# Linear attention and a routed two-layer network on one core: the first layer put ahead of the last routing step, subtractions moved to GpSimd, row loads and one output tile placed earlier

## The chip, the cores and the metric

The kernel runs on one core of a Trainium2 chip. A core has five engines that run side by side and meet through semaphores: TensorE (PE in the rows; its weight loads are PEld), VectorE (DVE), ScalarE (ACT), GpSimd (POOL) and SyncE (SP), which here only asks for transfers. The metric is the device time of one execution in microseconds.

## The reference

Attention with a feature map, then a mixture of eight experts with one expert for each token. Cut to what is computed:

```python
def phi(x):                                   # x: 4 x 8 x 576 x 64
    proj = einsum('bhsd,df->bhsf', x, w_phi)  # 128 features
    proj = proj - max(abs(proj), axis=-1)
    return concatenate([exp(proj), exp(-proj)], axis=-1)
kv, z = einsum('bhsf,bhsd->bhfd', phi(k), v), sum(phi(k), axis=2)
x = einsum('bhsf,bhfd->bhsd', phi(q), kv) / (einsum('bhsf,bhf->bhs', phi(q), z) + 1e-6)
# tokens: x as 2304 rows of 512
logits = x @ w_gate; e = argmax(logits); gate = softmax(logits)[e]
pos = how many earlier tokens chose e         # kept while pos < 576
h = maximum(rows_of_e @ w1[e], 0)             # 512 -> 1024
out = gate * (h @ w2[e])                      # 1024 -> 512
```

With this input the experts get 73, 516, 236, 236, 170, 250, 418 and 405 tokens.

## The kernel before

**Attention** goes through 72 items (`items`), 36 for each half of the tokens: a K item or a Q item is 128 tokens times four heads. `attention()` is a software pipeline written out by hand: in its step `t` every item that is in flight gets one stage. TensorE projects (L243, L244), VectorE takes the largest absolute value (L249) and subtracts it (L253, `center`), TensorE transposes a Q item (L329), ScalarE takes both exponentials (L331, L332), TensorE sums (L315 for K, L344 for Q), and `rows_out` divides by the sum. Nothing reorders this: each engine runs its instructions in the order in which the program emits them. Beside it, in later steps, ScalarE rounds the first expert's first-layer weights (`w_split`, L110, tile `h`), and VectorE or GpSimd takes the rest (L111, tile `l`): a product of two such pairs needs three matmuls. `x_split` does the same for the Q and K inputs (L179 on GpSimd).

**Routing** is done for groups of 9, 4, 3 and 2 blocks of 128 tokens (`route`). Its some twenty small steps lie in the queue `pending`, and `tick()` emits one or two of them between the large VectorE operations. After the first group thirteen more steps (`swaps`, L449 to L461) find the expert that leads so far and put it first. `positions` (L422) counts on TensorE. When a group is through, each block's rows are scattered to their expert's place in `xs` in DRAM (L426, an indirect transfer by GpSimd).

**Experts.** `prep` transposes a tile of 128 rows (L673, tile `pt`), ScalarE rounds it (L674), VectorE takes the rest (L675). `ffn1(f)` is the first layer for 128 of the 1024 hidden columns (L740, L741, L743), `relu` its result (L754, L757), `ffn2` the second layer for one tile of rows (L771, L773, L774; `py_t`, in the rows `pt` or `sm`), `put` scales it and scatters it to the output (L786, L153). `opening` begins with the leading expert, whose first 256 rows are surely there; `totals` (L907 to L913) writes the counts `cnt`, `count(e)` loads a count into a register of every engine, and branches choose the path: over 256 rows, over 128 (`to_two`), or fewer (`to_one`, which computes 128 rows with `thin1`). The second expert here has 73 rows and goes `to_one`, the four after it `to_two`. The first output tile of an expert (`first`) is computed behind the branch of the next one. `told` is a hint on where a branch will go. `loads` asks for the next expert's weights (L106, tile `raw`) and rows (L663, tiles `xi` and `xr`) from SyncE's queue, in which a request that waits holds up those behind it. `paced` ties a request to the latest VectorE operation.

Of the kernel before, what the change touches and what calls it, by code (L numbers as in the profile page):

```python
# [8 lines left out]
F32 = mybir.dt.float32  # L9
# [28 lines left out]
def tile_kernel(ctx: ExitStack, tc: tile.TileContext, qT, kT, vT, vv, w_phi, w_g, w1, w2, out, cap):  # L38
# [23 lines left out]
                   allow_small_or_imprecise_dtypes=True)  # L62
    tokid = cpool.tile([P, NT // P], I32, tag="tokid", name="tokid")
# [44 lines left out]
    def w_split(c, part, low=None):  # L108
        a, hi, lo = (t[:, :, part * P:(part + 1) * P] if c < 2 else t[:, part] for t in (raw_t[c], *w_t[c]))
        nc.scalar.activation(hi, a, AF.Copy)  # L110
        (low or nc.vector).tensor_tensor(lo, a, hi.bitcast(F32), ALU.subtract)  # L111
# [273 lines left out]
    def route(blk, n, xr, lg):  # L385
# [59 lines left out]
        def swaps():  # L445
# [7 lines left out]
                lambda: v.tensor_scalar(lead, lead8, float(NE), None, ALU.add),  # L453
                lambda: v.tensor_scalar(perm["h"], iota8, lead8, None, ALU.is_equal),
                lambda: v.tensor_scalar(perm["b"], perm["h"], lead, None, ALU.mult),
                lambda: v.tensor_scalar(perm["c"], iota8, float(-NE), lead, ALU.is_equal, ALU.mult),
                lambda: v.tensor_tensor(perm["d"], perm["c"], perm["b"], ALU.subtract),
                lambda: v.scalar_tensor_tensor(perm["e"], perm["d"], float(NE), iota8, ALU.add, ALU.add),
                lambda: v.tensor_scalar(perm["s"], perm["e"], float(slots), None, ALU.mult),
                lambda: v.tensor_copy(perm_i, perm["e"]),  # L460
                lambda: v.tensor_copy(seen_i, seen),  # L461
# [93 lines left out]
    def attention():  # L555
# [46 lines left out]
        depth = 8  # L602
        for t in range(len(items) + depth):
# [57 lines left out]
    def load_x(e, t0, t1, after):  # L661
        for s0, m in tiles[t0:t1]:
            dma = nc.sync.dma_start(xi_t[e % 2, s0][0:m], xs[e * slots + s0:e * slots + s0 + m, :])  # L663
            for w in after:
# [125 lines left out]
    def first(e):  # L790
        ffn2(wide, *tiles[0], 0)
        put(e, *tiles[0], 0)

    def ready(e):
        for t in tiles[:2]:
            prep(e, *t)
# [213 lines left out]
```

## Time and profile before

| what | us |
|---|---|
| median of 3 runs | 471.55 |
| lowest and highest run | 470.67 and 472.55 |
| the profiled execution | 467.43 |
| its span, first to last instruction | 465.7 |
| TensorE busy in the span | 412.6 (89%) |
| VectorE, ScalarE, GpSimd busy | 274.3, 245.6, 165.3 |

The profiled execution is 4.1 us (0.9%) under the median, and 1.7 us of it lie outside its span. Attention fills the span up to some 177 us, the opening goes to 220 us, the experts to 458 us. In the rows below a time is counted from the start of the span; an entry in square brackets is how long the engine sat idle before the row, and what ended that wait.

### The profile page before, as it was taken

The numbers are of one execution on the slowest core, as the hardware profiler recorded it, in microseconds if no ns is written. First come the engines' busy times: TensorE is split into PE (matmuls) and PEld (weight loads), VectorE is DVE, ScalarE is ACT, GpSimd is POOL, SyncE is SP. The second block draws the span as 40 slices with busy tenths as digits, with TensorE's granted clock in tenths as the row PEclk, the third lists the DMA queues.
The fourth block names the chain that finished last, engine by engine and source line by source line (L and its number), as shares of the span: only waits on it lengthen the run. The fifth ranks groups of instructions, "written<-read, shape, count | busy, mean of one in ns | idle before, by whom it ended". The sixth has DMA issues, their size and how long they took to land.

```text
span 465.7 us, 12137 instructions
## 1 busy us (share of the span) xinstructions
PE 412.6 (89%) x4777; PEld 362.9 (78%) x4777; DVE 274.3 (59%) x606; ACT 245.6 (53%) x453; POOL 165.3 (35%) x194
## 2 busy tenths in 40 slices
PE   6989999959998775846999599998989999999992
PEld 4778888848887664835988579896979899889872
DVE  5768887898976885521205857575656565165410
ACT  3879687667955663501215755554655554164310
POOL 1667486144677546000004510414123140042011
PEclk9999999998999997977999979999999999999997
DMA  7961698568056423195000769585775829310010
GB/s 266 383 258 45 209 368 288 198 212 292 10 168 199 161 112 152 56 333 164 24 24 27 249 241 309 193 307 201 259 240 208 304 73 326 115 34 24 0 48 27
DMA packets 42717, 82.80 MB, mean 178 GB/s; under 512 B 4351, under 2 KB 9343, under 8 KB 42624
## 3 DMA queue, kind: packets, MB, share of 16 engines
q1 hardware_dynamic: 38080, 72.13, 45.0%
q0 software_dynamic: 4544, 9.47, 5.8%
q8 instruction: 54, 0.88, 0.8%
q14 instruction: 39, 0.32, 0.2%
HBM read 62.65 MB, written 24.30 MB: 187 GB/s over the span
## 4 chain that ended last, share of the span: by engine, by line
PE 49%; DMA 4%; ACT 1%; issue 1%; POOLq 0%; SPq 0%; DVE 0%; POOL 0%; ACTq 0%
PE ph L741 7%; PE ph L743 7%; PE ph L740 7%; PE sm L771 5%; PE sm L773 4%; PE sm L774 4%; PE pt L771 3%; PE pt L773 3%; PE pt L774 3%; DMA xi<-xs 2%; PE pt L673 2%; DMA xr<-xs 2%; PE pt L769 1%; PE pt L767 1%; PE ph L718 1%
## 5 line engine op out<-in xcount | busy, mean ns | idle before, releaser
L179 POOL TENSOR_TENSOR stk<-px,stk 64x1024 f16<-64x1024 f32 (+1 forms) x30 | 70.8, 2361 | 58.7 <-ACT stk L178 58.1
L111 DVE TENSOR_TENSOR l<-raw,h 128x512 fp32r<-128x512 f32 x124 | 82.6, 701 | 8.4 <-ACT h L110 5.2
L153 POOL DMA_INDIRECT out<-y,it x22 | 21.6, 981 | 171.6 <-ACT y L786 95.5
L740 PE MATMUL ph<-xh,h 128*128 128x256 f32 (+3 forms) x272 | 76.5, 305 | 0.6 <-issue 0.6
L741 PE MATMUL ph<-xh,l 128*128 128x256 f32 (+3 forms) x272 | 76.2, 304 | 0.0
L110 ACT ACTIVATE h<-raw 128x512 fp32r<-128x512 f32 x128 | 74.6, 626 | 0.0
L757 DVE SCALAR_TENSOR_TENSOR h<-ph,h 128x256 fp32r<-128x256 f32 (+1 forms) x88 | 32.5, 392 | 54.8 <-ACT h L754 52.8
L754 ACT ACTIVATE h<-ph 128x256 fp32r<-128x256 f32 (+2 forms) x64 | 27.6, 431 | 60.5 <-PE ph L743 59.9
L249 DVE TENSOR_REDUCE m<-pr 128x4 f32<-128x512 f32 x72 | 49.2, 684 | 8.2 <-PE pr L244 4.7
L740 PEld LDWEIGHTS ph<-xh,h 128*128 128x128 f32 x272 | 52.8, 194 | 1.5 <-issue 0.6
L741 PEld LDWEIGHTS ph<-xh,l 128*128 128x128 f32 x272 | 52.9, 195 | 0.9
L253 DVE TENSOR_TENSOR d<-pr,m 128x512 f32<-128x512 f32 x72 | 49.8, 691 | 3.9
L743 PE MATMUL ph<-xh,h 128*128 128x256 f32 (+3 forms) x272 | 49.1, 303 | 0.0
L243 PE MATMUL pr<-whi,stk 128*128 128x128 f16 x260 | 37.0, 223 | 12.5 <-DVE d L253 11.6
L315 PE MATMUL acc<-v,kp 128*64 128x73 f32 (+1 forms) x1280 | 46.2, 234 | 0.4 <-issue 0.4
L315 PEld LDWEIGHTS acc<-v,kp 128*64 128x64 f32 (+1 forms) x1280 | 40.7, 140 | 5.0 <-issue 1.2
L344 PE MATMUL acc<-kv,qp 128*64 128x73 f32 x1152 | 44.5, 229 | 0.0
L344 PEld LDWEIGHTS acc<-kv,qp 128*64 128x64 f32 x1152 | 39.1, 136 | 6.0 <-issue 5.7
L743 PEld LDWEIGHTS ph<-xh,h 128*128 128x128 f32 x272 | 41.2, 195 | 0.7
L675 DVE TENSOR_TENSOR xh<-pt,xh 128x512 fp32r<-128x512 f32 (+1 forms) x23 | 14.9, 677 | 43.1 <-ACT xh L674 43.1
L771 PE MATMUL sm<-h,h 128*128 128x512 f32 x88 | 35.4, 403 | 3.2 <-ACT h L110 1.8
L244 PE MATMUL pr<-wlo,stk 128*128 128x128 f16 x260 | 36.5, 221 | 0.0
(143 smaller groups left out, 748.2 us busy)
## 6 DMA issues: line engine op xcount, KB each, us to landing
raw<-in_w SPq DMA_DIRECT2D x28, 1024.0 KB, 7.3
xs<-fill SPq DMA_DIRECT2D x18, 514.0 KB, 5.4
xr<-xs SPq DMA_DIRECT2D x24, 257.0 KB, 8.2
raw<-in_w SPq DMA_DIRECT2D x8, 512.0 KB, 4.3
vt<-in_vT SPq DMA_DIRECT2D x3, 1152.0 KB, 13.2
v<-in_vv SPq DMA_DIRECT2D x2, 1314.0 KB, 12.1
px<-in_kT SPq DMA_DIRECT2D x5, 512.0 KB, 9.5
px<-in_qT SPq DMA_DIRECT2D x4, 640.0 KB, 11.1
```

The costliest lines, as they stand in the source:

```text
L110: nc.scalar.activation(hi, a, AF.Copy)
L111: (low or nc.vector).tensor_tensor(lo, a, hi.bitcast(F32), ALU.subtract)
L179: return lambda: nc.gpsimd.tensor_tensor(t[other], x, t[own], ALU.subtract)
L243: nc.tensor.matmul(pr[:, j], lt, whi, start=True, stop=False)
L249: nc.vector.tensor_reduce(m.rearrange("p a b -> p (a b)"), pr, AX.X, ALU.max, apply_absolute_value=True)
L253: beat[0] = nc.vector.tensor_tensor(d, pr, m.to_broadcast([P, 4, NF]), ALU.subtract)
L315: nc.tensor.matmul(acc[f:f + D, a, j * GC:(j + 1) * GC], kp[lo:hi, j, a, f:f + D], vt[lo:hi, r, h * GC:(h + 1) * GC], start=first and j == ...
L344: nc.tensor.matmul(num[lo:hi, g, j * GC:(j + 1) * GC], qp[:, a, j, lo:hi], kv_t[b][:, a, 4 * g + j], start=(a == 0), stop=(a == 1))
L740: nc.tensor.matmul(acc, hi[:, k, fs], xh[:, k, o:o2], start=(k == 0), stop=False)
L741: nc.tensor.matmul(acc, lo[:, k, fs], xh[:, k, o:o2], start=False, stop=False)
L743: nc.tensor.matmul(acc, hi[:, k, fs], xl[:, k, o:o2], start=False, stop=(k == 3))
L771: nc.tensor.matmul(py[0:m], h_t[f][:, s0:s0 + m], hi, start=(f == 0), stop=False, skip_group_check=True)
```

## The change

Six things are moved. (1) Nine of the thirteen steps in `swaps` go from VectorE to GpSimd. (2) Of the first expert's eight first-layer weight subtractions in attention all go to GpSimd, each one step after its rounding; before, four were on VectorE and four on GpSimd, in the step of the rounding. (3) The two `prep` of attention come at steps 71 and 73 rather than 73 and 74, the loop ends four steps earlier, and the register load for the `again` branch comes at step 68. (4) `opening` emits three `ffn1` before the last `positions`; the second-layer weights are split in `spread`, `totals` comes after the sixth `ffn1`, and the rows of both the first and the second expert are asked for before the counts. (5) From then on rows are asked for ahead of weights (`ask`). (6) An expert's first output tile is computed in `between`, ahead of the next branch, with `prep` of the next expert in its middle; `to_two` and `to_one` share two full `ffn1` ahead of their inner branch, and the hints stand elsewhere.

The diff, cut:

```diff
@@ swaps
-                lambda: v.tensor_scalar(lead, lead8, float(NE), None, ALU.add),
...
-                lambda: v.tensor_copy(seen_i, seen),
+                lambda: gp.tensor_scalar(lead, lead8, float(NE), None, ALU.add),
...
+                lambda: gp.tensor_copy(seen_i, seen),
@@ attention
-        depth = 8
+        depth = 4
...
+            if 64 <= t < 72:
+                w_lo(*divmod(t - 64, 4), nc.gpsimd)
             if 63 <= t < 71:
-                c, part = divmod(t - 63, 4)
-                w_split(c, part, nc.gpsimd if part % 2 else nc.vector)
-            if t in (73, 74):
-                prep(0, *tiles[t - 73], ps_1.tile([P, 4, P], F32, tag="pt", name="pt"))
+                w_hi(*divmod(t - 63, 4))
+            if t == 68:
+                who["seen"] = nc.values_load(seen_i[0:1, 0:1], engines=engines, min_val=0, max_val=NT)
+                tc.mark_branch_hint_location("again", hint=who["seen"] < wide, engines=engines[:3])
+            if t in (71, 73):
+                prep(0, *tiles[(t - 71) // 2], ps_1.tile([P, 4, P], F32, tag="pt", name="pt"))
@@ experts
-    def first(e):
-        ffn2(wide, *tiles[0], 0)
+    def between(e):
+        ffn2(wide, *tiles[0], 0, range(5))
+        for f in range(2):
+            w_split(0, f)
+        for t in tiles[:2]:
+            prep(e + 1, *t)
+        for f in range(2, 8):
+            w_split(f // 4, f % 4)
+        ffn2(wide, *tiles[0], 0, range(5, 8))
         put(e, *tiles[0], 0)
...
+        prep_gi(e + 1)
+
+    def ask(e):
+        load_x(e, 0, 2, [] if e > 1 else row_dmas)
+        for c in range(2):
+            w_load(e, c)
+        load_x(e, 2, None, [])
@@ expert, to_one
             told(f"two{e}", cv[e] > P)
-            first(e - 1)
+            for f in range(2):
+                ffn1(f, f % 4, 0, wide)
             with tc.If(cv[e] > P, label=f"two{e}") as two:
...
+        for f in range(2):
+            relu(f, f % 4, 0, P)
+            loads(e, f)
+            w2_split(e, f)
+        for f in range(2, 9):
@@ opening
+    def spread(f):
+        if f >= 2:
+            relu(f - 2, (f - 2) % 4, 0, wide)
+        if f < 8:
+            w_hi(2 + f // 4, f % 4)
+        if 4 <= f:
+            w_lo(2 + (f - 4) // 4, f % 4, nc.vector)
...
-            for _ in range(4):
-                if pending:
+            for _ in range(6):
+                if pending and (f >= 2 or len(pending) > 1 or len(pending[0]) > AFTER):
                     step()
...
+            spread(f)
+            if f == 5:
+                assert not pending
+                totals()
...
+            if f == 5:
+                assert not scatters
+                load_x(0, 2, None, row_dmas)
+                ask(1)
```

Three places show how the instructions move. First GpSimd around step 40, where before only the subtractions `stk` of the inputs stood in a row:

```order
L192 TENSOR_TENSOR stk<-px,stk 64x1024
L466 TENSOR_SCALAR swap<-swap 128x1
L467 TENSOR_SCALAR permh<-iota_74,swap 128x8
L468 TENSOR_SCALAR permb<-permh,swap 128x8
L469 TENSOR_SCALAR permc<-iota_74,swap 128x8
L470 TENSOR_TENSOR permd<-permc,permb 128x8
L471 TENSOR_TENSOR perme<-permd,iota_76 128x8
L472 TENSOR_SCALAR perms<-perme 128x8
L192 TENSOR_TENSOR stk<-px,stk 64x1280
```

Seven of the nine steps stand ahead of the next `stk` (L192 is L179 of before). On VectorE, before, they stood between the reductions `m` and the subtractions `d` of attention:

```order
L452 TENSOR_REDUCE swap<-perma 128x1
L453 TENSOR_SCALAR swap<-swap 128x1
L253 TENSOR_TENSOR d<-pr,m 128x512
L454 TENSOR_SCALAR permh<-iota_74,swap 128x8
L455 TENSOR_SCALAR permb<-permh,swap 128x8
L249 TENSOR_REDUCE m<-pr 128x4
L456 TENSOR_SCALAR permc<-iota_74,swap 128x8
L457 TENSOR_TENSOR permd<-permc,permb 128x8
L253 TENSOR_TENSOR d<-pr,m 128x512
L458 SCALAR_TENSOR_TENSOR perme<-permd,iota_74 128x8
L459 TENSOR_SCALAR perms<-perme 128x8
```

Now three `d` and three `m` lie on VectorE between the last step that stays (`swap<-perma`) and `sel`, the first reader of `perms`.

Second TensorE at the end of attention. Before, the second tile's transposes, the last positions and the register load stood ahead of the first `ffn1`:

```order
L344 MATMUL acc<-kv,qp 64x73 x16
L673 MATMUL pt<-ident,xi 128x128 x4
L422 LDWEIGHTS tri
L422 MATMUL sm<-oh,tri 128x16
L422 LDWEIGHTS ones
L422 MATMUL sm<-rb,ones 128x16
L422 LDWEIGHTS ones
L422 MATMUL sm<-oh,ones 128x8
L960 TENSOR_LOAD seeni
L894 REGISTER_ALU
L1006 BRANCH_PREFETCH_HINT
L740 MATMUL ph<-xh,h_2700 128x256
```

Now the same positions (L435 is L422 of before) stand behind the third `ffn1`, whose last rows lead here:

```order
L760 MATMUL ph<-xh,l_2703 128x256
L762 MATMUL ph<-xh,h_2702 128x256 x4
L435 LDWEIGHTS tri
L435 MATMUL sm<-oh,tri 128x16
L435 LDWEIGHTS ones
L435 MATMUL sm<-rb,ones 128x16
L435 LDWEIGHTS ones
L435 MATMUL sm<-oh,ones 128x8
L759 MATMUL ph<-xh,h_2702 128x256
```

The transposes have moved ahead of the last sum of attention, and the register load into attention.

Third SyncE in the opening. Before, behind the branch on the counts, the next expert's first-layer weights came first, and then both experts' rows:

```order
L937 UNCONDITIONAL_BRANCH x2
L106 ISA
L106 DMA raw<-in_w 128x4x512
L106 ISA
L106 DMA raw<-in_w 128x4x512
L663 DMA xr<-xs 128x514 x2
L663 DMA xr<-xs 64x514
L663 DMA xr<-xs 128x514 x4
L663 DMA xr<-xs 64x514
```

Now, ahead of the counts, right behind the last half of the first expert's weights:

```order
L109 DMA raw<-in_w 128x2x512
L680 DMA xr<-xs 128x514 x2
L680 DMA xr<-xs 64x514
L680 DMA xr<-xs 128x514 x2
L109 ISA
L109 DMA raw<-in_w 128x4x512
L109 ISA
L109 DMA raw<-in_w 128x4x512
L680 DMA xr<-xs 128x514 x2
L680 DMA xr<-xs 64x514
```

The first expert's three late row tiles and two of the second expert's have moved ahead of its weights and of the register loads.

## Rows read from the trace of the kernel before

**Rows 1.** The page: TensorE's granted clock in 40 slices of 11.6 us, in tenths.
```profile
PEclk9999999998999997977999979999999999999997
```
**Rows 2.** Timeline, TensorE, steps 38 to 42: start, us, line, tile, wait before.
```profile
101.26 0.23 PE L243 MATMUL pr<-whi,stk 128*128 128x128 f16 x1 [0.33 <-DVE d L253]
105.54 0.23 PE L243 MATMUL pr<-whi,stk 128*128 128x128 f16 x1 [2.48 <-DVE d L253]
```
**Rows 3.** Timeline, VectorE and GpSimd, at the same place.
```profile
101.38 2.57 DVE L455 TENSOR_SCALAR permb<-permh,swap 128x8 f32<-128x8 f32 x1
...
95.15 0.20 POOL L472 COPY xr<-tokid 128x9 int32<-128x9 int32 x1 [1.29 <-DVE sm L468]
...
101.31 2.61 POOL L179 TENSOR_TENSOR stk<-px,stk 64x1280 f16<-64x1280 f32 x1 [3.75 <-ACT stk L178]
```
**Rows 4.** Timeline, TensorE: the same sum of 64 matmuls twice.
```profile
22.27 1.26 PE L315 MATMUL acc<-v,kp 64*64 64x73 f32 x64
...
106.23 2.23 PE L315 MATMUL acc<-v,kp 64*64 64x73 f32 x64
```
**Rows 5.** Waits over the whole span: us in total, times, longest us.
```profile
PE pr L243 <- DVE d L253: 11.6, 7, 3.1
```
**Rows 6.** Timeline, TensorE, VectorE, GpSimd, steps 63 to 65.
```profile
150.09 0.22 PE L243 MATMUL pr<-whi,stk 128*128 128x128 f16 x1 [1.40 <-DVE d L253]
...
147.65 1.07 DVE L111 TENSOR_TENSOR l<-raw,h 128x512 fp32r<-128x512 f32 x1 [2.56 <-ACT h L110]
...
150.90 1.30 POOL L111 TENSOR_TENSOR l<-raw,h 128x512 fp32r<-128x512 f32 x1
```
**Rows 7.** Timeline, TensorE, end of attention and first layer of the opening.
```profile
172.80 0.63 PE L329 MATMUL pt<-ident,d 128*128 128x128 f32 x4 [1.08 <-DVE sm L475]
...
181.97 0.19 PE L422 MATMUL sm<-oh,tri 128*128 128x16 bf16 x1 [4.54 <-DVE sm L479]
...
182.76 0.57 PE L740 MATMUL ph<-xh,h 128*128 128x256 f32 x1 [0.56 <-issue]
...
187.94 0.29 PE L740 MATMUL ph<-xh,h 128*128 128x256 f32 x1
```
**Rows 8.** Timeline, VectorE and TensorE: the counts, and what waits for them.
```profile
200.55 0.17 DVE L913 TENSOR_SCALAR cnt<-permb 128x8 int32<-128x8 f32 x1
...
202.61 0.77 PE L771 MATMUL pt<-h,h 128*128 128x512 f32 x1 [5.85 <-DVEq L937]
```
**Rows 9.** Timeline, GpSimd and TensorE: last scatter, transposes of late tiles.
```profile
185.60 0.97 POOL L426 DMA_INDIRECT xs<-xr,si  x1 [0.30 <-issue]
...
212.69 1.97 PE L673 MATMUL pt<-ident,xr 128*128 128x128 f32 x8 [4.62 <-DMA xr<-xs]
```
**Rows 10.** Chain of waits, 212 to 220 us: start, us, what.
```profile
213.84 0.61 ACT xh L674
214.47 0.70 DVE xh L675
...
217.48 0.43 PE pt L771
...
219.41 0.24 PE pt L771
```
**Rows 11.** Row loads (L663), 150 to 220 us; scatters over the span, from the page.
```profile
DMA to landing us min/median/max: 3.4/8.3/9.2
...
xs<-xr,si POOLq DMA_INDIRECT x18, 3.4
```
**Rows 12.** Timeline, TensorE, second and third expert; transposes at another join.
```profile
255.02 0.28 PE L718 MATMUL ph<-xh,h 128*128 128x256 f32 x1
...
268.88 1.97 PE L673 MATMUL pt<-ident,xi 128*128 128x128 f32 x8 [6.35 <-DMA xi<-xs]
...
294.35 1.03 PE L673 MATMUL pt<-ident,xr 128*128 128x128 f32 x8
```
**Rows 13.** Timeline, TensorE: one of two joins with a wait at the branch.
```profile
320.53 0.47 PE L771 MATMUL sm<-h,h 128*128 128x512 f32 x1 [1.84 <-ACT h L110]
```

More of the change, by code (lines that the diff above doesn't have):

```diff
@@ L106, in w_load, with w_parts, w_hi, w_lo @@
         return nc.sync.dma_start(raw_t[c][:, k0:k1], src.rearrange("o (k p) f -> p (o k) f", p=P)[:, k0:k1])
-    def w_split(c, part, low=None):
-        a, hi, lo = (t[:, :, part * P:(part + 1) * P] if c < 2 else t[:, part] for t in (raw_t[c], *w_t[c]))
+    def w_parts(c, part):
+        return (t[:, :, part * P:(part + 1) * P] if c < 2 else t[:, part] for t in (raw_t[c], *w_t[c]))
+    def w_hi(c, part):
+        a, hi, _ = w_parts(c, part)
         nc.scalar.activation(hi, a, AF.Copy)
-        (low or nc.vector).tensor_tensor(lo, a, hi.bitcast(F32), ALU.subtract)
+    def w_lo(c, part, engine):
+        a, hi, lo = w_parts(c, part)
+        engine.tensor_tensor(lo, a, hi.bitcast(F32), ALU.subtract)
+    def w_split(c, part):
+        w_hi(c, part)
+        w_lo(c, part, nc.vector)
     actx = ExitStack()
@@ L663, in load_x @@
             dma = nc.sync.dma_start(xi_t[e % 2, s0][0:m], xs[e * slots + s0:e * slots + s0 + m, :])
+            if e > 1 and not s0:
+                paced(dma)
             for w in after:
@@ L787, in put @@
         to_out(y[0:m], it[0:m])
[L790 to L798 removed]
+    def between(e):
[7 more added lines that the diff above has]
+        ffn2(wide, *tiles[0], 0, range(5, 8))
+        put(e, *tiles[0], 0)
+        prep_gi(e + 1)
[4 more added lines that the diff above has]
+        load_x(e, 2, None, [])
     def loads(e, f):
         if f == 0 and e + 1 < NE:
[L802 to L808 removed]
+            ask(e + 1)
     def later(e, todo, n):
@@ L860, in to_one @@
     def to_one(e):
-        for f in range(9):
+        for f in range(2):
[3 more added lines that the diff above has]
+        for f in range(2, 9):
             if f < 8:
@@ L864, in to_one @@
                 thin_sum(f)
-                loads(e, f)
-            if f:
+            if f > 2:
                 thin_relu(f - 1)
@@ L883, in expert @@
             told(f"two{e}", cv[e] > P)
-            first(e - 1)
+            for f in range(2):
+                ffn1(f, f % 4, 0, wide)
             with tc.If(cv[e] > P, label=f"two{e}") as two:
@@ L944, in opening @@
         told("many0", cv[0] > wide)
-        loads(0, 0)
-        ffn2(wide, *tiles[1], 1, range(4))
+        ffn2(wide, *tiles[1], 1, range(5))
         for t in tiles[2:]:
             prep(0, *t)
-        ffn2(wide, *tiles[1], 1, range(4, 8))
+        ffn2(wide, *tiles[1], 1, range(5, 8))
         prep_gi(0)
@@ L957, in opening @@
         with many.Else():
-            next_told(0)
-    few_seen = nc.values_load(seen_i[0:1, 0:1], engines=engines, min_val=0, max_val=NT)
-    told("again", few_seen < wide)
+            pass
+    AFTER = 10
+    few_seen = who["seen"]
     opening()
@@ L973, in tile_kernel @@
         if e + 1 < NE:
-            ready(e + 1)
-            prep_gi(e + 1)
-    first(NE - 1)
+            told(f"many{e + 1}", cv[e + 1] > wide)
+            between(e)
+    ffn2(wide, *tiles[0], 0)
+    put(NE - 1, *tiles[0], 0)
 def kernel(**inputs):
```

53 lines of the change are left out of this document (18 added, 35 removed).

## The prediction, made before the changed kernel ran

> **What bounds the kernel now.** I read the page first: TensorE is busy for 89% of the span, and its granted clock is clearly below full in few slices only, around 110 us, between 175 and 221 us, around 273 us, and in the last one, where TensorE has ended [rows 1]. Then the list of waits and TensorE's timeline with the idle time before each row: they show that the engine doesn't stand still all over the span but at some ten places, and each low clock stands behind one of them. So the kernel is bound by TensorE, and a change can gain what these waits and the slow stretches behind them cost, and little else. Where TensorE has no wait (110 to 145 us, 220 to 262 us, 270 to 450 us nearly throughout), work moved off another engine is worth nothing. The other engines' timelines then tell who is late at each wait.
>
> **Part 1, steps of the swap to GpSimd.** TensorE waits here twice for the subtraction d, 0.33 and 2.48 us [rows 2]. VectorE is late because a step on 8 columns took 2.57 us there, for just as long as GpSimd's subtraction beside it (101.31, 2.61 us) [rows 3]. Behind the wait a sum of 64 matmuls took 2.23 us that takes 1.26 us at full clock [rows 4]: 0.97 us. Together 3.8 us. Added are nine steps on GpSimd; a like small copy takes 0.20 us there [rows 3], so the seven ahead of `sel` make 1.4 us, against three d and three m that VectorE has to do meanwhile. They delay one `stk` subtraction by those 1.4 us, which is read many steps later. If GpSimd were late, VectorE would stand at `sel` with the next d behind it, and the gain would be zero. I take 3.5, bounds 0 and 3.8.
>
> **Part 2, weight subtractions to GpSimd.** VectorE's subtraction at 147.65 stood 2.56 us waiting for ScalarE's rounding, with the next m and d queued behind it, then ran 1.07 us, and TensorE's next projection waited 1.40 us [rows 6]. All waits of this kind come to 11.6 us in 7, the longest 3.1 us (at another place, not touched) [rows 5]; without that and the two of part 1 four are left, 5.7 us, one for each subtraction on VectorE. A step later the rounding is done, and on GpSimd no m stands behind it. GpSimd takes 1.30 us for one where VectorE took 1.07 [rows 6]; eight make 10.4 us over eight steps of some 2.2 us, beside other work of GpSimd's, so it has room, but not much. I take 5.7; bounds 0 (GpSimd sets the pace) and 7 (VectorE's freed time also shortens its later steps).
> The Trainium skill speaks against this move: its page "GPSIMD Engine Reference", section "Engine selection", gives elementwise work on two inputs to the Vector engine, with GpSimd about twice as slow. The rows agree in direction (1.30 against 1.07 us). Were the instruction's own length what counts, four moved ones would cost 4 x 0.23 = 0.9 us, and the sum below would be 6.6 us smaller; here what counts is what is queued behind it.
>
> **Part 3, the end of attention.** TensorE waits 1.08 us and then 4.54 us for the last routing steps before the positions [rows 7]. With three `ffn1` in front of the positions it has 3 x 1.47 = 4.4 us of work (at full clock six steps take the 8.8 us from 187.94 to the wait that ends at 202.61 [rows 7, 8]), nearly as long as the wait. So 5.6 us go. Against it: the first tile's transposes now stand between two users of the single `pt` buffer, whose next one waits for a ScalarE copy and a VectorE subtraction, 0.61 + 0.70 us [rows 10]; I count 1.5. The register load inside attention stands in front of every engine's work; I count 0.4, between 0 (most joins have the same load and no wait) and 1.84 [rows 13]. Net 3.7, bounds 2 and 5.6. And the clock: the first two `ffn1` took 5.18 us (182.76 to 187.94 [rows 7]) at half the rate; at full clock 2 x 1.47. That gives 2.2 more, if no long wait comes ahead of them.
>
> **Part 4, counts and late rows.** TensorE waits 5.85 us for the counts, since the six VectorE operations of `totals` stand behind eight subtractions; from cnt's end (200.72) to the next matmul are 1.9 us [rows 8]. With `totals` behind the sixth `ffn1` cnt is written while TensorE still computes, and those 1.9 us of loading and branching stay: gain 4.0, bounds 0 and 5.85. Then TensorE waits 4.62 us for row tiles that are asked for behind 2 MB of weights [rows 9]. Half the clock behind both waits: 18 matmuls of the second layer at 0.43 instead of 0.24 us [rows 10], 3.4 us, and eight transposes 1.97 instead of 1.03 us [rows 9, 12], 0.9 us. Together 8.9. Are the rows in time? The last scatter ended 4.6 us behind the positions (181.97 to 186.57 [rows 7, 9]). Positions now come 4.4 us into the first layer, so the last scatter starts 8.0 us into it, lands 3.4 us later, and an undisturbed row load takes 3.4 us [rows 11]: 14.8 us, with two tiles more asked behind it perhaps 16. The transposes are due at 8 x 1.47 + 1.9 + 15 x 0.24 = 17.3 us. That is in time by about 1 us; at the median landing of 8.3 us [rows 11] it would be late by 2.4. I take 8.9, bounds 0 and 8.9.
>
> **Part 5, rows ahead of weights, output tile ahead of the branch.** The third expert's rows come behind its weights, and TensorE waits 6.35 us [rows 12]: the second expert's path from 255.02 to 262.5 is the only one shorter than the transfer. Asked first, rows land while TensorE still does that path and the five `ffn2` parts that now precede `prep`. With the clock behind it (eight transposes 0.9 us, six matmuls 1.1 us) 8.4 us. Against it, the second expert's two full `ffn1` cost 1.47 each where thin ones take 7.5 / 8 = 0.94: 1.1 us. Net 7.3, bounds 0 and 7.5. For the other experts TensorE is full before and after; the tile only changes its place, and weights that land a row load later have the twenty-odd us of an expert's path.
> The inner branch now has two `ffn1` (2.9 us) between its hint and itself, before a whole `ffn2` tile of 24 matmuls (5.6 us). A branch that isn't ready costs what the worse of two joins shows, 1.84 us [rows 13]; I count one, 2.0, bounds 0 and 7 x 1.84 = 12.9.
>
> **The sum** is 3.5 + 5.7 + 3.7 + 2.2 + 4.0 + 8.9 + 7.3 - 2.0 = 33.3 us. The profiled execution would go from 467.43 to 434.1. It stands 4.1 us under the median of the runs, 471.55, which would go to 438.2; I give the medians from here on.
>
> **Rivals.** (a) Late rows: completion of the scatters or the loads is slower than my 14.8 us, and the wait and its clock stay: 438.2 + 8.9 = 447. For it: the median landing; against it: the request no longer stands behind weights. (b) GpSimd sets the pace in attention: `stk`, rows and scatters share its queue, parts 1 and 2 bring nothing: 438.2 + 9.2 = 447. Against it: ahead of a subtraction GpSimd stood 3.75 us waiting for ScalarE [rows 3]. (c) The inner branches aren't ready at any of seven experts: 12.9 in place of 2.0, 449. The Trainium skill has this as a rule (page "Runtime: NRT & Kernel Launch", section "Instruction fetch mechanics": a taken branch to a target that isn't near has to fetch it first); two of the joins here have such a wait and three none. (d) Slower than before: the same, but each inner branch costs the longest that TensorE stood at any branch, 5.85 us [rows 8]: 41 us in place of 2, 477. It decides from 35 / 7 = 5.0 us a branch on; against it: most of those 5.85 us were waiting for the counts. (e) Better: no branch waits, the register load is free and VectorE's freed time shortens attention more: 431. (f) The rewrite doesn't take effect, because VectorE still ends last at each wait: within 2 us of 471.55.
>
> **How the numbers follow.** Chances: the forecast (433 to 443) 0.52, better 0.12, late rows 0.12, GpSimd 0.08, branches 0.11, slower 0.03, no effect 0.02. The range that leaves out about 2 in 10 begins inside the better case, at 429, and ends behind case (c), at 450. What can be told from no change is about 0.5%, 2.4 us. Faster by more 0.95, within it 0.02, slower by more 0.03.
>
> **What would show it.** Right: no wait over 1 us before projections in steps 38 to 71; full clock throughout from attention to the first expert; positions within a few tenths behind the third `ffn1`; one wait of about 2 us at the counts and none at the late tiles; no wait for xi behind the second expert. Wrong: a VectorE wait at `sel` or a TensorE wait for a GpSimd `l`; a wait at the late tiles' transposes; waits of 1 to 2 us at the third `ffn1` of the experts.

## The result and the profile after

Beside the kernel before (472.05 us), the changed kernel took 443.88 us in the median of four runs, a ratio of 0.941 (95% interval 0.936 to 0.946): 28.2 us less, where 33.3 less had been forecast. 443.88 lies in the range (429 to 450), 5.7 us above the point and 0.9 us above the case that was given the chance of 0.52 (433 to 443). In two further groups of runs, on two chips and again beside the kernel before, the ratio was 0.938 (0.935 to 0.942) and 0.941 (0.937 to 0.945), gains of 29.2 and 28.1 us.

The first trace holds something that the second lacks. In the list of TensorE's waits (us in total, times, longest us) of the first trace (an execution of 446.0 us, span 444.2) one row stands in the first layer:

```profile
PE ph L759 <- DVE h L776: 2.8, 1, 2.8
```

Its timelines of VectorE and ScalarE at that place:

```profile
176.35 0.18 DVE L492 TENSOR_REDUCE sm<-sel 128x2 f32<-128x16 f32 x1
180.18 0.18 DVE L495 TENSOR_REDUCE sm<-es 128x2 f32<-128x16 f32 x1 [3.66 <-remote]
...
180.13 0.39 ACT L773 ACTIVATE h<-ph 128x256 fp32r<-128x256 f32 x1 [1.69 <-PE ph L762]
```

L495 reads the positions, whose matmuls had ended at 177.1, and L773 a layer step that ended at 178.7; both engines went on together at 180.13 to 180.18. In the second trace of the same kernel (label `again`, which is not the branch of that name; an execution of 439.41 us, span 437.7) the positions are read at once. TensorE's waits there, in total 1.3 us and more, and the row of its clock on the page:

```profile
PE pr L251 <- DMA px<-in_kT: 4.8, 1, 4.8
PE pr L256 <- DVE d L266: 3.1, 1, 3.1
PE ph L759 <- ACT h L116: 2.3, 2, 1.4
PE sm L790 <- ACT h L749: 2.1, 1, 2.1
PE pt L790 <- DVE l L120: 2.0, 1, 2.0
PE pt L342 <- DVE xh L694: 1.4, 1, 1.4
PE pt L793 <- DVEq L966: 1.3, 1, 1.3
```

```profile
PEclk9999999998999999979999899999999999999998
```

Against [rows 5]: the seven waits for d are one, and of the waits of 4 us and more in [rows 7 to 9, 12] none is left. Against [rows 1] (slices of 10.9 us here): the clock is lower at the same place near 100 us, in one slice near 190 and in one near 245 us, and, as before, in the last one, where TensorE has ended. I compare this second trace with the one of before (467.43 us, span 465.7), since neither has that stall. TensorE's timeline at the places of the terms:

```profile
169.41 0.39 PE L759 MATMUL ph<-xh,h 128*128 128x256 f32 x1
...
183.49 0.47 PE L790 MATMUL pt<-h,h 128*128 128x512 f32 x1 [2.02 <-DVE l L120]
...
185.46 0.79 PE L793 MATMUL pt<-h,h 128*128 128x512 f32 x1 [1.27 <-DVEq L966]
186.05 0.63 PE L790 MATMUL pt<-h,h 128*128 128x512 f32 x1
186.48 0.63 PE L792 MATMUL pt<-l,h 128*128 128x512 f32 x1
...
191.16 1.03 PE L692 MATMUL pt<-ident,xr 128*128 128x128 f32 x8
...
195.76 0.31 PE L759 MATMUL ph<-xh,h 128*128 128x320 f32 x1
...
230.81 0.28 PE L759 MATMUL ph<-xh,h 128*128 128x256 f32 x1
...
241.41 0.50 PE L790 MATMUL sm<-h,h 128*128 128x512 f32 x1 [2.06 <-ACT h L749]
...
249.51 0.28 PE L759 MATMUL ph<-xh,h 128*128 128x256 f32 x1
...
297.30 0.35 PE L759 MATMUL ph<-xh,h 128*128 128x256 f32 x1 [0.97 <-ACT h L116]
```

Two rows of before that [rows 1 to 13] lack, the first step at 320 columns and the third expert's first layer step:

```profile
219.95 0.31 PE L740 MATMUL ph<-xh,h 128*128 128x320 f32 x1
...
277.38 0.28 PE L740 MATMUL ph<-xh,h 128*128 128x256 f32 x1
```

From these the gain by stretch, each stretch ending at the row named:

| stretch of the span, up to | before, us | second trace, us | gained | forecast |
|---|---|---|---|---|
| first `ffn1` (182.76; 169.41) | 182.8 | 169.4 | 13.4 | 3.5 + 5.7 + 3.7 = 12.9 |
| first `ffn2` (202.61; 183.49) | 19.8 | 14.1 | 5.8 | 2.2 + 4.0 = 6.2 |
| `ffn1` at 320 columns (219.95; 195.76) | 17.3 | 12.3 | 5.1 | 8.9 |
| second expert's `ffn1` (255.02; 230.81) | 35.1 | 35.1 | 0.0 | 0 |
| third expert's `ffn1` (277.38; 249.51) | 22.4 | 18.7 | 3.7 | 7.3 |
| end of the span (465.7; 437.7) | 188.3 | 188.2 | 0.1 | -2.0 |
| all | 465.7 | 437.7 | 28.0 | 33.3 |

So attention as a whole came as forecast; what is missing is mostly in the late rows and in the second expert.

### The profile page after: what moved, and what is told of

The parts are those of the page before. It is cut to its first block, busy times and chain, and to the rows that moved or that the text cites. A ratio compares the mean times of both kernels' runs of the same rounds, so it can differ in the third digit from the quotient of the medians.

```text
span 444.2 us, 12112 instructions
## 1 busy us (share of the span) xinstructions
PE 411.7 (93%) x4785; PEld 361.1 (81%) x4785; DVE 265.8 (60%) x589; ACT 244.3 (55%) x451; POOL 171.8 (39%) x210
## 4 chain that ended last, share of the span: by engine, by line
PE 52%; ACT 1%; another core or an unknown queue 1%; DMA 1%; issue 0%; POOLq 0%; DVE 0%; ACTq 0%
PE ph L759 8%; PE ph L762 8%; PE ph L760 8%; PE sm L790 4%; PE sm L792 4%; PE sm L793 4%; PE pt L793 3%; PE pt L790 3%; PE pt L792 3%; PE pt L692 2%; PE pt L786 1%; PE pt L788 1%; PE ph L737 1%; ACT h L116 1%; PE ph L739 1%
## 5 line engine op out<-in xcount | busy, mean ns | idle before, releaser
L120 DVE TENSOR_TENSOR l<-raw,h 128x512 fp32r<-128x512 f32 x118 | 77.6, 686 | 26.3 <-ACT h L116 23.9
L166 POOL DMA_INDIRECT out<-y,it x22 | 23.9, 1088 | 178.0 <-issue 88.0
L192 POOL TENSOR_TENSOR stk<-px,stk 64x1024 f16<-64x1024 f32 (+1 forms) x30 | 70.9, 2362 | 50.3 <-ACT stk L191 49.5
L759 PE MATMUL ph<-xh,h 128*128 128x256 f32 (+3 forms) x280 | 78.5, 304 | 4.7 <-DVE h L776 2.8
L760 PE MATMUL ph<-xh,l 128*128 128x256 f32 (+3 forms) x280 | 77.9, 302 | 0.0
L116 ACT ACTIVATE h<-raw 128x512 fp32r<-128x512 f32 x128 | 75.8, 629 | 0.4 <-DMA raw<-in_w 0.4
L759 PEld LDWEIGHTS ph<-xh,h 128*128 128x128 f32 x280 | 54.0, 193 | 6.6 <-DVE h L776 3.0
L773 ACT ACTIVATE h<-ph 128x256 fp32r<-128x256 f32 (+3 forms) x66 | 28.3, 429 | 51.9 <-PE ph L762 49.2
L760 PEld LDWEIGHTS ph<-xh,l 128*128 128x128 f32 x280 | 54.2, 193 | 0.9
L776 DVE SCALAR_TENSOR_TENSOR h<-ph,h 128x256 fp32r<-128x256 f32 (+2 forms) x90 | 32.8, 387 | 34.7 <-ACT h L773 32.9
L762 PE MATMUL ph<-xh,h 128*128 128x256 f32 (+3 forms) x280 | 50.1, 301 | 0.0
L762 PEld LDWEIGHTS ph<-xh,h 128*128 128x128 f32 x280 | 42.0, 193 | 0.7
L344 ACT ACTIVATE qp<-pt 128x512 f32<-128x512 f32 x36 | 21.5, 597 | 26.9 <-PE pt L342 23.4
```

Of the source, the lines that this page charges most:

```text
L120: engine.tensor_tensor(lo, a, hi.bitcast(F32), ALU.subtract)
L192: return lambda: nc.gpsimd.tensor_tensor(t[other], x, t[own], ALU.subtract)
L759: nc.tensor.matmul(acc, hi[:, k, fs], xh[:, k, o:o2], start=(k == 0), stop=False)
L760: nc.tensor.matmul(acc, lo[:, k, fs], xh[:, k, o:o2], start=False, stop=False)
L762: nc.tensor.matmul(acc, hi[:, k, fs], xl[:, k, o:o2], start=False, stop=(k == 3))
```

## Experiments

Each group of four kernels below ran on one chip, beside the kernel before: `again` to `late_rows_behind` on a chip where before took 468.55 us, `rows_behind` to `totals3` where it took 471.24, `again2` to `best` where it took 472.57. The middle group has no changed kernel in it; by the ratios 0.938 and 0.941 it would take 442.1 to 443.4 there, an estimate on which the differences told for that group rest. Line numbers in the rows of an experiment are its own and can be off by two or three.

**The changed kernel a second time** (no edit).

> The changed kernel a second time. In its first trace VectorE stood 3.66 us behind the positions (L495), ScalarE's relu 1.69 us and TensorE then 2.77 us at the fifth step of the first layer, although the positions' matmuls had ended long before. Theory A: that stall is not in the order of the program and doesn't come again; then no TensorE wait over 1 us lies in the first layer, the clock there is full, and the span is some 3 us shorter than 444.2. Theory B: it belongs to the new order (the result of the positions is told late when a layer step follows on TensorE); then the 3 us wait stands at the same place again.

439.4 us (438.6 to 442.2), ratio 0.938. Theory A: TensorE has no wait inside the first layer, and the span is 6.5 us shorter than 444.2. From the first `ffn1` to the first `ffn2` are 14.1 us against 17.8, 3.7 us less for the stall and the slow clock behind it. Another 3.1 us lie in attention, where the first trace has short waits of TensorE that end with no releaser.

**The swap's steps back on VectorE.**

```diff
-                lambda: gp.tensor_scalar(lead, lead8, float(NE), None, ALU.add),
+                lambda: v.tensor_scalar(lead, lead8, float(NE), None, ALU.add),
...
```

> Only the nine steps of the swap are put back on VectorE. Forecast's step 1: 3.5 us are lost, 447.4 against 443.9, with waits of about 0.3 and 2.5 us for d back on TensorE. Rival: the gain was small, because in the changed kernel sel on VectorE took 1.32 us beside a GpSimd subtraction and the half clock of that place stayed; then it is within 1 us of 443.9.

442.06 us, ratio 0.942 (0.939 to 0.946): 2.7 us more than `again` by the medians. TensorE's, VectorE's and GpSimd's timelines show the old picture again, row for row that of [rows 2, 3]:

```profile
101.14 0.23 PE L256 MATMUL pr<-whi,stk 128*128 128x128 f16 x1 [0.33 <-DVE d L266]
105.42 0.23 PE L256 MATMUL pr<-whi,stk 128*128 128x128 f16 x1 [2.48 <-DVE d L266]
...
101.26 2.58 DVE L468 TENSOR_SCALAR permb<-permh,swap 128x8 f32<-128x8 f32 x1
...
101.19 2.62 POOL L192 TENSOR_TENSOR stk<-px,stk 64x1280 f16<-64x1280 f32 x1 [3.75 <-ACT stk L191]
```

The step on 8 columns began 0.07 us behind GpSimd's subtraction and ended 0.03 us behind it, 103.84 against 103.81: it stood for as long as GpSimd worked. From the wait at 97 us to the first `ffn1` this kernel needs 75.0 us, `again` 71.9: 3.0 us, near the forecast's 3.5. But the two waits alone are 2.8 us, and the slow clock that the forecast counted with them (0.97 us) is there in both kernels, only at another place: in `swap_dve` behind the second wait (granted clock 0.64 from 105 to 109 us), in `again` some 6 us earlier, behind the wait at 97 us (0.52 from 99.4 to 102.5 us). There a sum of 32 matmuls took 2.19 us that otherwise takes 1.25:

```profile
100.34 2.19 PE L328 MATMUL acc<-v,kp 128*64 128x73 f32 x32
```

**The first layer's weight subtractions back in the rounding's step.**

```diff
-            if 64 <= t < 72:
-                w_lo(*divmod(t - 64, 4), nc.gpsimd)
             if 63 <= t < 71:
-                w_hi(*divmod(t - 63, 4))
+                c, part = divmod(t - 63, 4)
+                w_hi(c, part)
+                w_lo(c, part, nc.gpsimd if part % 2 else nc.vector)
```

> Only the eight subtractions of the first layer's weights go back to where they were: in the rounding's own step, every other one on VectorE. Forecast's step 2: 5.7 us are lost (449.6), as four waits of 1.3 to 1.6 us for d ahead of projections. Rival: with the swap off VectorE there is room for them, and what stood behind the rounding is now shorter; then fewer than two such waits come back and it is within 2 us of 443.9.

445.83 us, ratio 0.948 (0.945 to 0.952): 6.4 us more than `again`. Its timeline of TensorE has the four waits back:

```profile
150.38 0.21 PE L256 MATMUL pr<-whi,stk 128*128 128x128 f16 x1 [1.40 <-DVE d L266]
156.34 0.22 PE L256 MATMUL pr<-whi,stk 128*128 128x128 f16 x1 [1.59 <-DVE d L266]
162.11 0.22 PE L256 MATMUL pr<-whi,stk 128*128 128x128 f16 x1 [1.26 <-DVE d L266]
168.16 0.22 PE L256 MATMUL pr<-whi,stk 128*128 128x128 f16 x1 [1.68 <-DVE d L266]
```

They add up to 5.9 us; the forecast said 5.7, with this mechanism.

**The first expert's late rows behind weights.**

```diff
-                load_x(0, 2, None, row_dmas)
-                ask(1)
+                for c in range(2):
+                    w_load(1, c)
+                load_x(0, 2, None, row_dmas)
+                load_x(1, 0, None, [])
```

> Only the first expert's late row tiles are asked for behind the 2 MB of weights again, at the place in the first layer where the changed kernel asks for them. Forecast's step 4, second half: a wait of about 4.6 us ahead of the late tiles' transposes comes back, with half the clock behind it, 8.9 us in all (452.8). Rival: the request itself comes some 13 us earlier than in the kernel before, so that rows behind weights are in time as well; then no wait over 1.5 us and within 1 us of 443.9. Between them (2 to 5 us): the wait comes back, the clock doesn't fall.

438.07 us, ratio 0.934 (0.930 to 0.938): 1.3 us less than `again`, not more. SyncE's queue says why. Of this kernel, and then of `again` (each row the time of the first request, how long the requests took to be issued, their number):

```profile
154.09 12.00 SPq L109 DMA_DIRECT2D raw<-in_w  x4
181.57 4.99 SPq L680 DMA_DIRECT2D xr<-xs  x8
186.82 1.05 SPq L109 DMA_DIRECT2D raw<-in_w  x2
```

```profile
154.34 4.40 SPq L109 DMA_DIRECT2D raw<-in_w  x2
181.46 2.50 SPq L680 DMA_DIRECT2D xr<-xs  x5
184.16 0.98 SPq L109 DMA_DIRECT2D raw<-in_w  x2
```

The rows wait for the scatters and are asked for at 181.5 in either order. The weights wait for nothing but a free buffer: ahead of the rows they are asked for by 166, behind them at 184. Transposes wait for no transfer in either. So the rival is right: what made the rows punctual is the place of the request, in the first layer instead of behind the counts; the order against the weights is worth nothing here (the two intervals overlap).

**The third to eighth expert's rows behind weights.**

```diff
-            if e > 1 and not s0:
-                paced(dma)
...
     def ask(e):
-        load_x(e, 0, 2, [] if e > 1 else row_dmas)
+        if e == 1:
+            load_x(e, 0, 2, row_dmas)
         for c in range(2):
-            w_load(e, c)
-        load_x(e, 2, None, [])
+            dma = w_load(e, c)
+            if e > 1 and c == 0:
+                paced(dma)
+        load_x(e, 0 if e > 1 else 2, None, [])
```

> Only the order of the requests of the third to eighth expert is undone: their first two row tiles are asked for behind their 2 MB of weights again. Forecast's step 5: the wait for xi behind the second expert comes back, 6.4 us and the slow clock behind it, some 7 us more than the changed kernel. Rival: in the kernel before the rows landed some 12.2 us after the request; in the changed kernel the request is made at about 234.3 us of its second trace and the transposes come at 246.6, since two full layer steps, a wait of 2.1 us and five parts of the second layer stand between; then rows behind weights are just in time too, and the time is within 1.5 us of the changed kernel.

445.45 us, ratio 0.945 (0.942 to 0.948): 2 to 3 us more than the changed kernel would take there. The view of tile `xi` gives the landing of the row loads, first of `again`, then of this kernel:

```profile
DMA to landing us min/median/max: 3.1/4.0/5.2
```

```profile
DMA to landing us min/median/max: 3.4/8.3/10.3
```

They land 4.3 us later, yet no transpose waits:

```profile
252.66 1.04 PE L690 MATMUL pt<-ident,xi 128*128 128x128 f32 x8
257.26 0.36 PE L757 MATMUL ph<-xh,h 128*128 128x256 f32 x1 [1.48 <-ACT h L116]
```

The second expert's stretch is 20.4 us (from 236.9 to 257.3) against 18.7 in `again`, but the first trace of the changed kernel has 20.5 there (236.49 to 256.96) with no edit. From the second expert's first step to the end of the span this kernel needs 207.4 us, the changed kernel 207.7, 206.9 and 206.4 in its three traces. So the traces show no loss at the place of the edit, and where the 2 to 3 us come from is not shown. The 6.35 us of [rows 12] don't come back: two full layer steps and five parts of the second layer ahead of `prep` give the transfer its time even in the old order.

**The last positions ahead of the first layer**, first without and then with the changed kernel beside it on the chip.

```diff
-        depth = 4
+        depth = 8
```

> Only the last routing steps are put back ahead of the first layer (all of them in the attention loop). Forecast's step 3: a wait of about 4.5 us ahead of the positions and half the clock in the first two layer steps come back, 5.9 us in all beyond the changed kernel (5.6 of waits, 2.2 of clock, less 1.9 of cost that stays). Rival: the wait comes back, but the clock doesn't fall, or the scatters ending earlier take back a part: 2 to 4 us.

> The last routing steps ahead of the first layer again, now beside the changed kernel on the same chip. Forecast's step 3: 5.9 us more than the changed kernel. Rival, from the first measurement of this edit: the wait (4.0 us) and the slow clock behind it come back, but the counts and the late rows come earlier against the first layer, so the waits there go: within 2 us.

442.97 us (ratio 0.942, 0.938 to 0.946), 0 to 1 us more than the changed kernel would take there; then 447.12 (0.946, 0.942 to 0.950) against 444.44 (0.941) beside it, 2.7 us more, with intervals that overlap. TensorE's and VectorE's timelines of the second:

```profile
176.45 0.18 PE L435 MATMUL sm<-oh,tri 128*128 128x16 bf16 x1 [4.02 <-DVE sm L492]
...
181.02 0.42 DVE L776 SCALAR_TENSOR_TENSOR h<-ph,h 128x256 fp32r<-128x256 f32 x1 [2.97 <-issue]
```

The wait is back nearly in full (4.0 us; in `again` TensorE doesn't wait for the last positions at all). But both chips have the stall, and here it falls on VectorE's first relu, where TensorE doesn't wait; in the changed kernel it costs 2.8 us. Against `again2` the first layer starts 2.9 us later, counted from the wait at 97 us, and takes 3.2 less (14.6 against 17.9); behind it the part up to the step at 320 columns takes 1.6 less (9.6 against 11.1), so that this kernel is 1.9 us ahead there. The profiled execution loses that and more where nothing was edited: 1.4 us ahead of the wait at 97 us and 2.2 from the second expert on. So on chips with the stall the traces show no price of the old order, though the medians are 0 to 3 us higher. The price without the stall wasn't measured: no experiment confirms the 5.9 us forecast for this step.

**The inner branch's hint without a lead.**

```diff
-            told(f"two{e}", cv[e] > P)
             for f in range(2):
                 ffn1(f, f % 4, 0, wide)
+            told(f"two{e}", cv[e] > P)
```

> Only the hint of the inner branch is moved from two layer steps (2.9 us) ahead of it to directly ahead of it, at all seven experts. Forecast's rival (c): a branch that isn't ready costs up to 1.84 us, 12.9 us for seven. Theory: the hint's lead isn't what decides, as the second trace of the changed kernel has no wait at any inner branch and its two waits of 0.97 and 1.36 us stand at outer ones: within 1.5 us of the changed kernel.

444.49 us, ratio 0.944 (0.941 to 0.948): 1 to 2.5 us more than the changed kernel would take, well short of 12.9. In its waits the two at branches are shorter than in `again`, not longer, and both stand ahead of an expert's first layer step, not of its third:

```profile
PE ph L759 <- issue: 1.2, 2, 0.6
```

From the second expert's first step to TensorE's last matmul it needs 196.9 us, `again` 198.0. The edit moves one hint, that of `two`, which five of the seven experts meet; the two with 418 and 405 tokens take the branch over 256 rows, whose inner hint stays where it was. So at five inner branches nothing is lost that shows, with or without a lead, and rival (c) is out; a branch without any hint was not run.

**Totals two layer steps earlier.**

```diff
-            if f == 5:
+            if f == 3:
                 assert not pending
                 totals()
```

> The changed kernel, with the totals and the counts two layer steps earlier (behind the fourth, not the sixth). In the second trace of the changed kernel the last step of the counts, on 8 columns, took 2.03 us on VectorE beside a GpSimd subtraction (0.17 us in the kernel before), four relu-and-subtraction pairs are queued behind it, and TensorE waits 2.02 and 1.27 us for VectorE at the counts. Theory: the neighbour on GpSimd does it, as at the swap; earlier, the step meets no subtraction, takes under 0.3 us, both waits together shrink to 1.5 us at most and the slow clock behind them goes: 2 to 4 us less than the changed kernel. Rival: the waits are the register loads and the branch, which come after the counts wherever they are made: within 1 us.

442.6 us, ratio 0.937 (0.933 to 0.941): within 1 us by the median; the two waits at the counts are still 1.3 and 1.2, as in the changed kernel's other two traces. The reason to expect more was a row of VectorE in `again`, here with GpSimd's beside it:

```profile
179.59 2.03 DVE L931 TENSOR_SCALAR cnt<-permb 128x8 int32<-128x8 f32 x1
...
179.04 2.55 POOL L120 TENSOR_TENSOR l<-raw,h 128x512 fp32r<-128x512 f32 x2
```

In `totals3` that step takes 0.43 us. But GpSimd's pair then stops another:

```profile
183.76 2.80 DVE L120 TENSOR_TENSOR l<-raw,h 128x512 fp32r<-128x512 f32 x1
...
183.44 2.56 POOL L120 TENSOR_TENSOR l<-raw,h 128x512 fp32r<-128x512 f32 x2
```

In each case VectorE's instruction ends with the pair (181.62 against 181.59) or about its own length behind it (186.56 against 186.00; usually 0.68 us). The theory is right on what slows the step, but the step is not what TensorE mainly waits for: with it at 0.43 us here and at 1.23 in `again2` (186.95, beside one subtraction) the waits are the same 1.3 and 1.2 us, against 2.02 and 1.27 in `again`. VectorE's queue ahead of the branch is as long as it was.

**The changed kernel a third time.**

> The changed kernel a third time, as the measure for the three kernels beside it on the same chip. In its first trace, and in three of four kernels that ran together on another chip, TensorE stood 2.7 to 3.0 us in the first layer; in the four kernels of the batch of its second trace not at all. Theory A: the stall goes with the chip (time some 3 us longer where it stands, the kernel before 2 to 3 us longer too); then this trace shows either the stall and some 443 us, or none and some 439 us. Theory B: it comes and goes from execution to execution; then the time and the stall don't go together with the time of the kernel before.

444.44 us, ratio 0.941, and the stall: 2.8 us in the list of waits (L759 for L776). Together with the chips above this fits theory A (of this run), as far as one trace of each kernel goes: on the chip without the stall before takes 468.55 and the changed kernel 439.4, on those with it 471.2 to 472.6 and 444.

**Four of the second layer's subtractions behind the branch at the counts.**

```diff
         for f in (8, 9):
-            spread(f)
-        for part in (2, 3):
-            w_lo(3, part, nc.gpsimd)
-        for c in (2, 3):
-            w_load(1, c)
+            relu(f - 2, (f - 2) % 4, 0, wide)
...
         told("many0", cv[0] > wide)
+        for part in range(4):
+            w_lo(3, part, nc.vector if part < 2 else nc.gpsimd)
+        for c in (2, 3):
+            w_load(1, c)
```

> The changed kernel with the last four subtractions of the first expert's second weights (two on VectorE, two on GpSimd) moved from ahead of the counts' branch to behind it. Theory: at the counts TensorE waits for VectorE's queue, in which a step on 8 columns stood 2.03 us beside GpSimd's pair of subtractions, and two relu-and-subtraction pairs more than needed; without them the two waits (2.02 and 1.27 us) come to 1.5 us at most, the half clock behind them goes, 2 to 4 us less than the changed kernel. Rival: the waits are register load and branch alone, as the kernel with the counts two steps earlier still waited 1.3 and 1.2 us: within 1 us.

441.37 us, ratio 0.931 (0.927 to 0.935) against 0.941 (0.937 to 0.945) of `again2`: the intervals don't overlap, 3.1 us less by the medians. TensorE's timeline:

```profile
189.98 0.50 PE L790 MATMUL pt<-h,h 128*128 128x512 f32 x1 [1.28 <-ACTq L962]
190.31 0.40 PE L792 MATMUL pt<-l,h 128*128 128x512 f32 x1
190.55 0.39 PE L793 MATMUL pt<-h,h 128*128 128x512 f32 x1
...
193.53 1.03 PE L692 MATMUL pt<-ident,xr 128*128 128x128 f32 x8
```

The requests for the second expert's second-layer weights move with them. The wait ahead of L793 is gone, and the matmuls behind it follow each other every 0.23 us (granted clock 1.00), not 0.43 (0.51) as at 186 us of `again`. From the first `ffn2` to the transposes are 3.6 us; `again2` took 6.6 (190.1 to 196.7). One wait of 1.28 us stays, ended by ScalarE's branch.

**The same, and a shorter queue in the second expert.**

```diff
             if f > 2:
                 thin_relu(f - 1)
-                w2_split(e, f - 1)
+                if f < 6:
+                    w2_split(e, f - 1)
+        for f in range(5, 8):
+            w2_split(e, f)
...
```

The cut part of the diff is the edit of `lo_late` and the order of requests of `late_rows_behind`.

> The kernel lo_late with two more edits: in the short path of the second expert the last three splits of the second weights come behind the last relu, and the second expert's first weights are asked for ahead of the first expert's late rows. Theory: the wait of 2.06 us at the second expert's output is queueing on ScalarE and VectorE behind those splits and goes below 1 us with the slow clock behind it (2 us), and the weights bring 0.6 to 1.3: 3 us less than lo_late. Rival: the splits are then late at the output tile itself, and the wait only moves: equal to lo_late within 1 us.

439.24 us (437.1 to 441.3), ratio 0.929 (0.925 to 0.933): the fastest version, 5.2 us under the changed kernel beside it. Its gain over `lo_late`, 2.1 us, is within the intervals. The second expert is not where it comes from:

```profile
PE sm L790 <- ACT h L116: 2.7, 1, 2.7
```

The wait is 2.7 us instead of 2.1, and it now ends with one of the roundings that were put behind the last relu, though the first matmul reads none of these; why it waits for them is not shown. The size says little, since the same wait is 2.7 us in the first trace and 3.4 in `positions_first2`. The stretch is as long as before (18.5 us; `lo_late` 18.7). So the rival was right on the wait: it moved. In the traces 1.5 of the 2.1 us lie in the first layer (16.4 us against 17.9), where the half clock that `lo_late` has near 184 us doesn't come; which edit does that, if one does, is open.

## Why the prediction was right, point by point

**Part 1, swap: the waits right, the clock not.** 3.5 forecast, 3.0 in the trace of `swap_dve` against `again`, 2.7 in the medians. GpSimd's seven steps stood at 100.85 to 103.22, 2.4 us where the forecast had 1.4, and VectorE didn't wait for them. The sum of 64 matmuls is back at 1.26 us [rows 4], but the 0.97 us counted for it were not gained: the slow stretch came some 6 us earlier, as told above.

**Part 2, weight subtractions: right, and for the reason given.** 5.7 forecast, 5.9 in waits and 6.4 in medians when undone. The instruction on GpSimd is longer, and it doesn't matter. It is longer by more than the forecast said: the 1.07 us of VectorE in [rows 6] were not its own length, since the median of its 124 such subtractions before is 0.69 us. This one, too, stood beside GpSimd,

```profile
147.13 1.04 POOL L382 TENSOR_TENSOR xr<-nb,rd 128x512 f32<-128x512 f32 x1 [0.89 <-ACT nb L381]
```

and ended 0.55 us behind it (148.72 against 148.17). The other three did the same (1.03 to 1.12 us, each 0.55 behind). So the move also took away some 0.4 us of contention at each of four places, which the forecast had not seen.

**Part 3, end of attention: right by the sum, on the chip without the stall.** The stretch up to the first `ffn1` gave 13.4 for 12.9; less 3.0 and 5.9 for the parts above, 4.5 are left for the 3.7. The 1.5 us for `prep` between two users of `pt` were 1.41 (the wait of L342 above), the 0.4 for the register load can't be seen. The wait ahead of the last positions is gone, as three layer steps were to cover all of it, and the first layer's steps follow at 1.44 us, so that 1.9 of the clock's 2.2 came as well. Where the stall falls into the first layer, the new order shows no gain over the old one (`positions_first2`).

**Part 4, counts: mis-sized.** 4.0 forecast; 5.85 us became 2.02 + 1.27 in `again`, a gain of 2.6. The failing step is "cnt is written while TensorE still computes, and those 1.9 us of loading and branching stay": cnt was written at 181.62, when TensorE's last layer step had just ended (181.48), since its last step stood 2.03 us beside GpSimd's subtractions, 0.17 in [rows 8]. The change had put two of those there; I had counted the neighbour's price at the swap, where it was to be removed, and not where the same change added one. That cost at most 0.8 us, as the traces with a shorter step have 1.3 + 1.2. More came from the four pairs of relu and subtraction behind cnt, ahead of VectorE's branch: in `lo_late`, with two of VectorE's subtractions and GpSimd's two behind the branch, one wait of 1.28 stays.

**Part 4, late rows: the wait right, the reason and the size wrong.** The wait of 4.62 us is gone. But it wasn't the order against weights, as `late_rows_behind` shows, and of 8.9 us 6.3 came (5.1 in the table, and 1.27 of the waits just told, which lie in this stretch). What is missing is the clock: it fell behind the waits at the counts (0.51 from 186.0 to 191.2 us), and twelve matmuls ran at 0.43 us instead of 0.23 (186.05 and 186.48 above), 2.4 us. I had put the whole slow clock of this stretch on the late rows' wait, though the wait for the counts stands first and kept its share; `lo_late`, with one wait of 1.28 us there, has full clock behind it.

**Part 5: the wait right, the price of the new cover wrong.** The 6.35 us for xi are gone, and the rows needn't come first for it: in `rows_behind` the wait stays away, so the gain belongs to the output tile and the layer steps that now stand ahead of `prep`. 3.7 us came instead of 7.3. The failing step is "rows land while TensorE still does that path", in which I looked only at TensorE: on ScalarE the first relu comes 0.8 us late (233.18) behind six roundings and an output tile's scaling, and a short step takes 1.0 us there and on VectorE where TensorE takes 0.93, so that TensorE stands 2.06 us at the end of it and loses 1.8 us to the slow clock behind that (241.41 above; granted clock 0.61 from there to 245.8; the first `ffn2` to the third expert takes 8.1 us, where 15 + 9 matmuls and eight transposes are 6.3 at full clock).

**The inner branches: mis-sized, to the good.** 2.0 counted; the end of the span has 0.1 us gained, with two waits at outer branches still there (0.97 and 1.36; before 1.84 [rows 13] and 1.33). The sentence of the Trainium skill behind rival (c) (page "Runtime: NRT & Kernel Launch", section "Instruction fetch mechanics", on taken branches) has no case here: with the hint directly ahead of them, five inner branches still cost nothing that shows, and the two waits left at outer ones in `again` end with ScalarE's roundings.

Of the rivals, (a) late rows, (b) GpSimd as the bound, (d) and (f) are out by the traces, and no chip reached the 431 us of (e). The 5.3 us by which the traces fall short of 33.3 are the three mis-sized terms (1.4 + 2.6 + 3.6) and 0.3 of the first steps' clock, less 2.1 at the branches and 0.5 in attention. So the total came as near as it did partly by luck: three terms were 7.6 us too large, and the price counted for the branches made up 2.1 of it. Of the signs named beforehand, full clock throughout up to the first expert failed (7 tenths near 190 us), and at the counts there are two waits where one was named.

## What to carry to other kernels

When a change moves work to another engine, look at every place where that engine will now be busy, and ask which small instruction of its neighbour stands beside it: the contention that was removed at one place was put back at another by the same edit. And ask what stands in each engine's queue ahead of a branch, not only when the value that the branch needs is ready. The wait at the counts, cut from 5.85 us to 2.02 and 1.27, kept its slow clock; so a clock's gain is booked only when the first long wait of its stretch goes, and even then it can turn up behind another wait, as it did at the swap. Rows that had to wait for a producer lost nothing here to weights that were asked for ahead of them and waited for nothing.

## What the runs showed of the hardware

Some VectorE instructions don't run slowly beside GpSimd's subtractions, they look stopped: three of usually 0.17, 0.17 and 0.68 us took 2.58, 2.03 and 2.80 and ended with GpSimd's work or about their own length behind it, and in two of them that was two subtractions in a row. It needn't be: in `lo_late` the same subtraction beside such a pair took 1.74 us, and GpSimd's pair 2.98 in place of 2.55, so VectorE got in between the two.

```profile
187.82 1.74 DVE L120 TENSOR_TENSOR l<-raw,h 128x512 fp32r<-128x512 f32 x1
...
187.73 2.98 POOL L120 TENSOR_TENSOR l<-raw,h 128x512 fp32r<-128x512 f32 x2 [2.97 <-ACT h L773]
```

Others beside the same kind of work ran at their usual length (0.42 us for the relu at 183.42 in `totals3`). The Trainium skill has this as a rule (page "SBUF — State Buffer", section "Who interferes with whom": one pair of ports that VectorE and GpSimd share, under an exclusive lock); the rows here agree. Whether VectorE stays locked out over two GpSimd instructions or gets in between isn't said there.

In the first trace and in all eight on two chips VectorE or ScalarE stood some 2 to 4 us in the first layer, until 178 to 181 us, in whichever order the positions came, and attention was 1 to 4 us longer as well (73.1 to 75.8 us from the wait at 97 us to the first `ffn1` where the edit leaves it alone, 71.9 in `again`); on the third chip of the experiments in none of four kernels, one trace each. What makes it is open: no view shows who held the result back.
